# Row maxima of a softmax brought across partition quadrants: VectorE copies in place of a selector product on TensorE

## The chip, the cores and the metric

The kernel runs on one core of a Trainium2 chip. The metric is the device time of one execution in microseconds. Before the change it is 1114.38 us, the median of three runs (1112.85 to 1114.99).

## The reference

Attention with keys and values pooled over 4x4 windows, followed by a soft mixture of experts on its output. Sizes: B = 4 batches, N = 12288 queries per batch, C = 128 channels, 768 pooled keys per batch, 8 experts with 4 slots each.

```python
kv_pool = kv.reshape(B, H // r, r, W // r, r, C).mean(axis=(2, 4))
k = v = kv_pool.reshape(B, -1, C) @ w_sr
s = scale * (q @ k.transpose(0, 2, 1))
s = s - s.max(-1, keepdims=True)
a = np.exp(s)
a /= a.sum(-1, keepdims=True) + 1e-09
attn = a @ v
...
logits = x @ phi            # x: the attention's output, 49152 rows
d = softmax of logits over the rows;   slots = d.T @ x
slot_out = relu(slots @ w1) @ w2       # per expert
c = softmax of logits over the slots;  out = c @ slot_out
```

The maximum that matters here is `s.max(-1)`: one number per query, over its 768 keys.

## The kernel before, in words

The 49152 queries are worked through in 96 blocks of 512. A block's scores are computed transposed: TensorE multiplies six tiles of 128 keys with the 512 queries, in three products each (high and low parts of both operands, L473 to L475), so that keys lie on the partitions and queries along the free dimension. The six tiles fill three double banks of PSUM (s0 to s2).

The maximum over the keys is then a maximum across partitions. It is found in steps on VectorE:

- rowmax1, L480, three times per block: a transposing reduction of a double bank. It transposes 32x32 squares and takes the maximum along 32 keys. What comes out has, on partition j of quadrant k (a quadrant is a group of 32 partitions), for each of the block's 16 groups of 32 queries (NBK = 16) the maximum over the 32 keys that lie in quadrant k, for query j of the group.
- rowmax2, L490 and L492: the maximum over the six tiles (96 to 16 elements per partition, written to the top of a PSUM bank), then a product with `quad`, a 0/1 table, that spreads the 16 values of each quadrant into a slot of its own: 64 elements per partition, three quarters of them zeros.
- rowmax_pe, L500: TensorE multiplies these 128x64 values with `sel`, a 128x128 table of zeros and ones that adds up the partitions of equal number within their quadrant. Since only one of the four is not zero in each slot, every partition gets all four quadrants' maxima. It is an fp32 product, which the profile shows as two matmuls and two weight loads.
- rowmax3, L505: the maximum over the four slots (64 to 16 elements).
- rowmax4, L510: a transpose of 32x32 squares, which spreads the result so that every key's partition holds the maximum of each of the 512 queries (tile mb).

Then VectorE subtracts mb from the scores in four instructions (L518, tile t), which frees the double banks for the next block's products; ScalarE takes the exponential twice, to fp16 (phi, L525) and to fp32 (L529); GpSimd takes the difference of the two as a low part (plo, L534); and TensorE multiplies with the values in 72 matmuls (L551, L552, L559). GpSimd also splits the queries (qlo, L463). Every four blocks a group's logits are worked into a running softmax over the rows on all engines. After the last block comes the experts' part and the output.

The order of the instructions on TensorE, VectorE, ScalarE and GpSimd is written out by a planner (class Plan). Each step has an engine, a cost, a latency after it, a due time, the steps it needs and the buffers that it takes and gives back; the planner goes through time and always issues the most urgent step that can start. Due times of a block count from T0 = HEAD + i * PER. A step marked hot is waited for, up to HOLD = 0.7 us, instead of starting another on its engine. The steps of the maximum are hot: r2 (L935), pe (L936), r3 (L937), r4 (L938). Two PSUM banks (ring "m") are shared by the products with the values, the key and value projections, the groups' small products and the selector product; the planner lets the latter use the top of a bank beside a product with the values (key "pq").

Each engine executes its instructions in the order that the planner gave them, and waits at each for the results that it needs.

Of the kernel before, what the change touches and what calls it, by code (L numbers as in the profile page):

```python
# [11 lines left out]
F16 = mybir.dt.float16  # L12
U32 = mybir.dt.uint32
AF = mybir.ActivationFunctionType
ALU = mybir.AluOpType
X = mybir.AxisListType.X
# [3 lines left out]
P = 128  # L20
EPS = 1e-9
PK = 16.0
KSPLIT = 512
VK = 4096.0
Q32 = 32
# [7 lines left out]
class Plan:  # L33
# [13 lines left out]
    def op(self, eng, cost, lat, prio, deps, fn, acq=(), use=(), at=0.0, slack=0.0, hot=False, raw=0.0):  # L47
        n = len(self.ops)
        if eng != "PE" and any(ring == "m" for ring, _ in use):
            prio -= URGE  # L50
        for key in list(acq) + list(use):
            self.users.setdefault(key, []).append(n)
        self.ops.append((eng, cost, lat, prio, list(deps), fn, list(acq), at, slack, hot, raw, list(use)))
        return n
# [117 lines left out]
def attention_then_soft_moe(ctx: ExitStack, tc: tile.TileContext, qT, kv0, kvT, w_sr, w_srT, phi, w1, w2, outT):  # L172
    nc = tc.nc
    B, C, NQ = qT.shape
    R2, NK = kvT.shape[2], kvT.shape[3]
    NT = NK // P
    NS = phi.shape[1]
    E, _, FF = w1.shape
# [3 lines left out]
    BQ = 512  # L182
# [16 lines left out]
    TH = NT // NH  # L199
    PB = 5  # L200
# [7 lines left out]
    sp = es.enter_context(tc.tile_pool(name="sp", bufs=2))  # L208
# [16 lines left out]
        out=mask, in_=ident.rearrange("p (t e j) -> p e t j", t=TS, e=E), axis=XY, op=ALU.add  # L225
# [10 lines left out]
    NQD = P // Q32  # L236
    sel1 = cp.tile([P, Q32], F32, tag="sel1", name="sel1")
    nc.vector.tensor_reduce(out=sel1, in_=ident.rearrange("p (k j) -> p j k", k=NQD), axis=X, op=ALU.add)
    sel = cp.tile([P, P], F32, tag="sel", name="sel")
# [3 lines left out]
    quad = cp.tile([P, NQD], F32, tag="quad", name="quad")  # L243
# [14 lines left out]
    qsp = {}  # L258
    S = {}
    MX = {}  # L260
    PQ = {}
    TT_ = {}
    PP = {}
    PX = {}
# [3 lines left out]
    NBK = BQ // Q32  # L268
    NU = NT // 2

    plan = Plan({
        "m": 2, "t": TBUF, "phi": PB, "plo": PB, "q": 2, "qs": 2, "xl": 2, "D": 1, "kv": 2,
        "pooled": 1, "v32": 1, "r6": 2, "rq": 2, "m1": 2, "mb": 1, **{f"s{u}": 1 for u in range(NU)},
    })
    op = plan.op

    banks = [pm.tile([P, 512], F32, tag=f"m{b}", name=f"m{b}") for b in range(2)]
# [1 line left out]
    def mt(shape, name):  # L279
        return banks[plan.bank]  # L280

    PER = 9.8
    KLAG = 6
    KV0 = 14.5
    KVS = 1.0
    QKP = 5
# [197 lines left out]
        )  # L484

    def rowmax2(i):
        top = banks[plan.bank][:, 512 - (NQD + 1) * NBK :]
        pq = PQ[i] = top[:, NBK:]
        r1 = top[:, :NBK]
        nc.vector.tensor_reduce(out=r1, in_=MX[i].rearrange("p t b -> p b t"), axis=X, op=ALU.max)  # L490
        rq = sp.tile([P, NQD, NBK], F32, tag="rq", name=f"rq_{i}")
        nc.vector.tensor_tensor(  # L492
            out=rq, in0=r1.unsqueeze(1).broadcast_to([P, NQD, NBK]),
            in1=quad.unsqueeze(2).broadcast_to([P, NQD, NBK]), op=ALU.mult,
        )
        MX[i] = rq

    def rowmax_pe(i):
        pqv = PQ.pop(i)
        nc.tensor.matmul(pqv, sel, MX[i].rearrange("p k b -> p (k b)"), start=True, stop=True)  # L500
        MX[i] = pqv

    def rowmax3(i):
        m1 = sp.tile([P, NBK], F32, tag="m1", name=f"m1_{i}")
        nc.vector.tensor_reduce(out=m1, in_=MX[i].rearrange("p (k b) -> p b k", k=NQD), axis=X, op=ALU.max)  # L505
        MX[i] = m1

    def rowmax4(i):
        m = sp.tile([P, BQ], F32, tag="mb", name=f"mb_{i}", bufs=1)
        nc.vector.transpose(out=m, in_=MX[i].unsqueeze(2).broadcast_to([P, NBK, Q32]))  # L510
        MX[i] = m
# [9 lines left out]
        )  # L521

    def exp_hi(i, h):
        hi = PP[i, h] = sp.tile([P, TH, BQ], F16, tag="phi", name=f"phi_{i}_{h}", bufs=PB)
        nc.scalar.activation(hi, TT_[i, h], AF.Exp, bias=lnk, scale=SCALE)  # L525

    def exp_t(i, h):
# [3 lines left out]
    def plo(i, h):  # L531
        lo = sp.tile([P, TH, BQ], F16, tag="plo", name=f"plo_{i}_{h}", bufs=PB)
        eng = nc.vector if i == NB - 1 else nc.gpsimd
        eng.tensor_tensor(out=lo, in0=TT_.pop((i, h)), in1=PP[i, h], op=ALU.subtract)  # L534
        PP[i, h] = (PP[i, h], lo)

    def av_tile(i, k):
        if k % 2 == 0 and i == NB - 1:
# [6 lines left out]
    def av_hi(i, k):  # L545
        _, vhi, vlo = VU[i // BPB]
        px = av_tile(i, k)
        ks = slice(k * P, (k + 1) * P)
        for t in range(NT):
            p = PP[i, t // TH][0][:, t % TH, ks]  # L550
            nc.tensor.matmul(px, p, vhi[:, t, :], start=(t == 0), stop=False)  # L551
            nc.tensor.matmul(px[:, 1:], p, vlo[:, t, :], start=False, stop=False)  # L552

    def av_lo(i, k):
        vhi = VU[i // BPB][1]
        px = PX[i, k // 2][:, k % 2, :]
        ks = slice(k * P, (k + 1) * P)
        for t in range(NT):
            nc.tensor.matmul(px, PP[i, t // TH][1][:, t % TH, ks], vhi[:, t, :], start=False, stop=(t == NT - 1))  # L559
# [195 lines left out]
    def dve(n):  # L755
        return n / 960 + 0.07
# [15 lines left out]
    ops = {}  # L772
# [19 lines left out]
    for n, which in enumerate(LOADS):  # L792
        dep = [] if n < 2 else [ops["pool", 0, 6 * (n - 1) - 2]]
        loaded.append(op("SP", 0.3, 0, 0, dep, lambda which=which: start_kv(which)))
        for h, e0, cnt in which:
            for c in range(e0, e0 + cnt, 2):
# [4 lines left out]
                    acq=[("t", ("pool", h))] if c == 0 else [], use=[("t", ("pool", h))] if c else [],  # L801
# [96 lines left out]

    def av_rest(i, k, m, p, prev):
        los = [ops["lo", i, 0], ops["lo", i, 1]]  # L900
        a2 = op("PE", 6 * 0.072, 0.17, p + 0.8, prev + los, lambda: av_lo(i, k), use=[("plo", (i, 0)), ("plo", (i, 1)), m])
        if k % 2:
            g = GOF[i]
            first = i == GB[g][0] and k == 1
            x = ("xl", g)
            ops["x", i, k // 2] = op(
                "DVE" if i == NB - 2 and k == 1 else "ACT", act(2 * VW) + (0.1 if i == NB - 2 and k == 1 else -0.03), 0.1, p - 2, [a2] + evs[-1:], lambda: av_evac(i, k // 2),
                acq=[x] if first else [], use=[m] + ([] if first else [x]),
            )
            evs.append(ops["x", i, k // 2])  # L910
        return [a2]
# [3 lines left out]
    for i in range(NB):  # L915
        b, ib = divmod(i, BPB)
        T0 = HEAD + i * PER
# [5 lines left out]
        kd = [ops["k", b, 0], ops["k", b, 1]]  # L923
        for t in range(NT):
            u = t // 2
            ops["qk", i, t] = op(
                "PE", 3 * 0.2315, 0.17, T0 - QKP + 0.65 * t, [ops["ql", i]] + kd[: 1 if t < KSPLIT // P else 2] + ([ops["qk", i, t - 1]] if t else [ops["qk", i - 1, NT - 1]] if i else []),
                lambda i=i, t=t: qk(i, t), acq=[(f"s{u}", i)] if t % 2 == 0 else [], use=[("qs", i)] + ([(f"s{u}", i)] if t % 2 else []),
            )
            if t % 2:  # L930
                ops["r", i, u] = op(
                    "DVE", dve(2 * BQ) + 0.02, 0.08, T0 - 2.0 + 0.65 * t, [ops["qk", i, t], ops["qk", i, t - 1]] + ([ops["r", i, u - 1]] if u else []),
                    lambda i=i, u=u: rowmax1(i, u), acq=[("r6", i)] if u == 0 else [], use=[(f"s{u}", i)] + ([("r6", i)] if u else []),
                )
        r2 = op("DVE", 0.36, 0.08, T0 + 2, [ops["r", i, NU - 1]], lambda i=i: rowmax2(i), acq=[("m", ("pq", i)), ("rq", i)], use=[("r6", i)], hot=True, raw=0.14)  # L935
        pe = op("PE", 0.27, 0.3, T0 - 10, [r2], lambda i=i: rowmax_pe(i), use=[("m", ("pq", i)), ("rq", i)], hot=True)  # L936
        r3 = op("DVE", 0.12, 0.08, T0 - 10, [pe], lambda i=i: rowmax3(i), acq=[("m1", i)], use=[("m", ("pq", i))], hot=True)  # L937
        r4 = op("DVE", dve(BQ) - 0.03, 0.08, T0 - 10, [r3], lambda i=i: rowmax4(i), acq=[("mb", i)], use=[("m1", i)], hot=True, raw=0.14)  # L938
        for t, n in ((0, 2), (2, 1), (3, 1), (4, 2)):
            h, o2 = divmod(t, TH)  # L940
            ops["s", i, t] = op(
                "DVE", dve(n * BQ), 0.08, T0 - 4 + 0.63 * t, [r4] + ([ops["s", i, t0]] if t else []), lambda i=i, t=t, n=n: sub(i, t, n),
                acq=[("t", (i, h))] if o2 == 0 else [], use=[(f"s{t // 2}", i), ("mb", i)] + ([("t", (i, h))] if o2 else []),
                raw=0.0 if t else 0.14,
# [3 lines left out]
        for h in range(NH):  # L948
# [5 lines left out]
                acq=[("plo", (i, h))], use=[("t", (i, h)), ("phi", (i, h))],  # L954
            )
            ops["hi", i, h] = e1
        prev = [ops["hi", i, 0], ops["hi", i, 1], ops["t", b, 0], ops["t", b, 1]] + ([ops["av", i - 1]] if i else []) + ([ops["g7m", GOF[i] - 2]] if i == GB[GOF[i]][0] and GOF[i] > 1 else [])
        los = [ops["lo", i, 0], ops["lo", i, 1]]
        pp = [("phi", (i, 0)), ("phi", (i, 1))]
        pl = [("plo", (i, 0)), ("plo", (i, 1))]  # L960
        end = i == NB - 1
        px = [(f"s{k // 2}" if end else "m", ("px", i, k // 2)) for k in range(TB)]
        for k in range(TB):
            m = px[k]
            p = T0 + AVD * PER + 1.3 * k
            a1 = op("PE", 12 * 0.0705, 0.17, p, prev + ([] if end else los), lambda i=i, k=k: av_hi(i, k), acq=[m] if k % 2 == 0 else [], use=pp + ([m] if k % 2 else []))
            ops["hv", k] = prev = [a1]
            if not end:
                prev = av_rest(i, k, m, p, prev)
        if end:  # L970
            for k in range(TB):
                prev = av_rest(i, k, px[k], T0 + AVD * PER + 6, prev)
        a2 = prev[0]
# [28 lines left out]
    for g in range(len(GB)):  # L1002
        n = nt(g) * NS
        p = HEAD + (GB[g][0] + GB[g][1] + KLAG) * PER
# [230 lines left out]
```

## Time and profile before

| | |
|---|---|
| median of three runs | 1114.38 us |
| the profiled execution's own time | 1114.22 us |
| its span, first to last instruction | 1112.4 us |
| TensorE, VectorE busy, share of the span | 94%, 89% |
| ScalarE, GpSimd busy, share of the span | 74%, 78% |

A group's line in the profile reads: line of the kernel, engine, operation, what is written and read, shapes (partitions x elements), number of instructions, then busy time in us and mean ns of one, then the idle time of the engine just before them and what ended it. PE is TensorE, PEld its weight loads, DVE VectorE, ACT ScalarE, POOL GpSimd. In the view of waits a line names who waited for whom, the total, how many times and the longest. In the timeline a row has its start and its length in us. The view of busy time by window has one column per engine, in the order PE, PEld, DVE, ACT, POOL, then the granted clock, the busy share of the DMA engines and GB/s.

### The profile page before, as it was taken

Reading aid. Unit: us, or ns where it says so; the run is one execution under the profiler, and the core shown is the slowest. Engines: PE = TensorE matmul, PEld = TensorE weight load, DVE = VectorE, ACT = ScalarE, POOL = GpSimd, SP = SyncE. Lnnn points to the kernel's source line nnn. Section 1 sums busy time; section 2 is a strip of 40 time slices with the busy share of each in tenths; the row PEclk is TensorE's granted clock in tenths of the full one; section 3 lists DMA queues with packets and bytes.
Section 4 is the critical chain, followed back from the end, with each engine's and each line's share of the span. In section 5 each row is a group of like instructions: output and inputs, shape, how many; then the busy total and the mean of one; then the engine's idle time right before and its main releaser. Section 6 shows DMA issues by size and latency. Waiting matters only on the chain.

```text
span 1112.4 us, 24632 instructions
## 1 busy us (share of the span) xinstructions
PE 1046.7 (94%) x10198; PEld 897.3 (81%) x10198; DVE 984.9 (89%) x1492; ACT 822.7 (74%) x1006; POOL 866.2 (78%) x480
## 2 busy tenths in 40 slices
PE   3699999999999999999999999999999999997876
PEld 2588888888888888888888888888888888886343
DVE  7899889889889989899899988989989988987895
ACT  1677778778778778878877788688788777875563
POOL 0579897788899888789889889779889889773340
PEclk9799999999999999999999999999999999999885
DMA  9315421111125310120136210120110110113398
GB/s 342 117 22 132 96 44 39 39 58 39 39 54 124 91 42 22 39 70 27 39 83 123 71 53 1 39 96 2 39 39 1 39 39 2 39 39 115 141 407 360
DMA packets 17407, 89.15 MB, mean 80 GB/s; under 512 B 1680, under 2 KB 3984, under 8 KB 11152
## 3 DMA queue, kind: packets, MB, share of 16 engines
q1 hardware_dynamic: 13408, 69.47, 16.8%
q0 software_dynamic: 3312, 17.70, 8.4%
q8 instruction: 81, 1.33, 0.5%
q10 hardware_dynamic: 576, 0.41, 0.1%
q14 instruction: 30, 0.25, 0.1%
HBM read 58.87 MB, written 25.17 MB: 76 GB/s over the span
## 4 chain that ended last, share of the span: by engine, by line
PE 67%; DVE 27%; issue 2%; ACT 2%; POOL 1%; DMA 1%; SPq 0%; DVEq 0%; ACTq 0%; POOLq 0%
PE m L551 11%; PE m L552 10%; PE m L559 10%; PE s L473 9%; PE s L475 9%; PE s L474 9%; DVE t L518 8%; DVE r L480 8%; PE m L500 3%; PE m L690 2%; DVE mb L510 2%; PE po L1120 2%; DVE o L1129 2%; DVE cm L628 1%; DVE pool L311 1%
## 5 line engine op out<-in xcount | busy, mean ns | idle before, releaser
L534 POOL TENSOR_TENSOR plo<-t,phi 128x1536 f16<-128x1536 f32 x190 | 595.8, 3143 | 125.1 <-ACT t L529 123.8
L525 ACT ACTIVATE phi<-t,lnk 128x1536 f16<-128x1536 f32 x192 | 301.6, 1571 | 133.5 <-DVE t L518 132.9
L480 DVE TRANSPOSE_TENSOR_REDUCE r<-s 128x32 f32<-128x1024 f32 x288 | 349.8, 1236 | 27.1 <-PE s L475 21.1
L551 PE MATMUL m<-vhi,phi 128*128 128x161 f16 x2280 | 354.5, 234 | 2.5 <-DVE m L505 1.3
L552 PE MATMUL m<-vlo,phi 128*128 128x160 f16 x2280 | 353.5, 233 | 0.0
L518 DVE TENSOR_TENSOR t<-s,mb 128x1024 f32<-128x1024 f32 (+1 forms) x384 | 342.9, 949 | 8.8 <-DVE mb L510 0.9
L529 ACT ACTIVATE t<-t,lnk 128x1536 f32<-128x1536 f32 x192 | 299.8, 1568 | 2.3
L551 PEld LDWEIGHTS <-phi 128*128 128x128 f16 x2304 | 227.0, 99 | 22.9 <-issue 22.8
L473 PE MATMUL s<-qhi,khi 128*128 128x512 f32 x576 | 238.1, 413 | 6.5 <-DVE t L518 6.1
L552 PEld LDWEIGHTS <-phi 128*128 128x128 f16 x2304 | 225.5, 98 | 5.2 <-issue 3.3
L475 PE MATMUL s<-qhi,klo 128*128 128x512 f32 x576 | 227.2, 394 | 0.0
L474 PE MATMUL s<-qlo,khi 128*128 128x512 f32 x576 | 226.6, 393 | 0.0
L559 PE MATMUL m<-vhi,plo 128*128 128x161 f16 x2280 | 221.9, 233 | 0.3 <-POOL plo L534 0.3
L559 PEld LDWEIGHTS <-plo 128*128 128x128 f16 x2304 | 174.8, 100 | 1.3 <-issue 0.6
L463 POOL TENSOR_TENSOR qlo<-q,qhi 128x512 fp32r<-128x512 f32 x96 | 125.7, 1310 | 26.9 <-ACT qhi L459 26.9
L569 ACT ACTIVATE xl<-m 128x322 f32<-128x322 f32 x189 | 81.0, 428 | 76.1 <-PE m L559 75.7
L473 PEld LDWEIGHTS s<-qhi,khi 128*128 128x128 f32 x576 | 109.7, 190 | 29.9 <-issue 3.6
L475 PEld LDWEIGHTS s<-qhi,klo 128*128 128x128 f32 x576 | 109.2, 190 | 24.6 <-DVE klo L353 0.5
L474 PEld LDWEIGHTS s<-qlo,khi 128*128 128x128 f32 x576 | 109.8, 191 | 20.3 <-issue 0.7
L510 DVE STREAM_TRANSPOSE mb<-m 128x512 f32<-128x512 f32 x96 | 68.3, 711 | 3.3
L459 ACT ACTIVATE qhi<-q 128x512 fp32r<-128x512 f32 x96 | 59.2, 617 | 2.4 <-issue 1.0
L505 DVE TENSOR_REDUCE m<-m 128x16 f32<-128x64 f32 x96 | 21.5, 224 | 40.5 <-PE m L500 40.5
(140 smaller groups left out, 854.1 us busy)
## 6 DMA issues: line engine op xcount, KB each, us to landing
q<-qT SPq DMA_DIRECT2D x23, 1024.0 KB, 4.8
outT<-o SPq DMA_DIRECT2D x21, 1024.0 KB, 5.2
kva<-kvT POOLq DMA_DIRECT2D x9, 1536.0 KB, 11.4
kva<-kvT SPq DMA_DIRECT2D x3, 1536.0 KB, 10.5
kv<-kv SPq DMA_DIRECT2D x8, 512.0 KB, 5.7
w<-w SPq DMA_DIRECT2D x2, 1536.0 KB, 6.4
w<-w SPq DMA_DIRECT2D x4, 768.0 KB, 4.6
outT<-o SPq DMA_DIRECT2D x6, 512.0 KB, 4.3
```

The lines of the kernel that those rows point to most:

```text
L463: nc.gpsimd.tensor_tensor(out=lo, in0=q_src(i), in1=hi.bitcast(F32), op=ALU.subtract)
L473: nc.tensor.matmul(s, khi[:, ks], hi, start=True, stop=False)
L474: nc.tensor.matmul(s, khi[:, ks], lo, start=False, stop=False)
L475: nc.tensor.matmul(s, klo[:, ks], hi, start=False, stop=True)
L480: nc.vector.tensor_reduce(out=MX[i][:, 2 * u : 2 * u + 2, :].rearrange("p t b -> p (t b)"), in_=S[i, u].rearrange("p t (b j) -> p (t b) j" ...
L518: nc.vector.tensor_tensor(out=TT_[i, h][:, o : o + n, :], in0=S[i, t // 2][:, u : u + n, :], in1=MX[i].unsqueeze(1).broadcast_to([P, n, BQ ...
L525: nc.scalar.activation(hi, TT_[i, h], AF.Exp, bias=lnk, scale=SCALE)
L529: nc.scalar.activation(t, t, AF.Exp, bias=lnk, scale=SCALE)
L534: eng.tensor_tensor(out=lo, in0=TT_.pop((i, h)), in1=PP[i, h], op=ALU.subtract)
L551: nc.tensor.matmul(px, p, vhi[:, t, :], start=(t == 0), stop=False)
L552: nc.tensor.matmul(px[:, 1:], p, vlo[:, t, :], start=False, stop=False)
L559: nc.tensor.matmul(px, PP[i, t // TH][1][:, t % TH, ks], vhi[:, t, :], start=False, stop=(t == NT - 1))
```

## The change

The product with `quad` and the selector product are gone. L490 writes its 16 maxima into slot 0 of an SBUF tile rq on all 128 partitions. Three copies on VectorE bring the values of partitions 32 to 63, 64 to 95 and 96 to 127 down to slots 1, 2 and 3 of partitions 0 to 31. Four reductions on VectorE then each read the four slots of partitions 0 to 31 and write their maximum to one of the four quadrants of m1. The transpose L510 follows as before. TensorE has no part in the maximum any more, and nothing of it lies in the shared PSUM banks.

The planner's table follows: the step pe is gone, r2, r3 and r4 have new costs, the period of the due times PER is 9.5 instead of 9.8, and the assumed costs of the products are slightly lower. The handle of a block's phi (PP) becomes a pair from the start, so that the last block's first products may be issued ahead of its low parts.

```diff
-    PER = 9.8
+    PER = 9.5
...
     def rowmax2(i):
-        top = banks[plan.bank][:, 512 - (NQD + 1) * NBK :]
-        pq = PQ[i] = top[:, NBK:]
-        r1 = top[:, :NBK]
-        nc.vector.tensor_reduce(out=r1, in_=MX[i].rearrange("p t b -> p b t"), axis=X, op=ALU.max)
         rq = sp.tile([P, NQD, NBK], F32, tag="rq", name=f"rq_{i}")
-        nc.vector.tensor_tensor(
-            out=rq, in0=r1.unsqueeze(1).broadcast_to([P, NQD, NBK]),
-            in1=quad.unsqueeze(2).broadcast_to([P, NQD, NBK]), op=ALU.mult,
-        )
+        nc.vector.tensor_reduce(out=rq[:, 0, :], in_=MX[i].rearrange("p t b -> p b t"), axis=X, op=ALU.max)
+        for k in range(1, NQD):
+            nc.vector.tensor_copy(rq[:Q32, k, :], rq[k * Q32 : (k + 1) * Q32, 0, :])
         MX[i] = rq
-
-    def rowmax_pe(i):
-        pqv = PQ.pop(i)
-        nc.tensor.matmul(pqv, sel, MX[i].rearrange("p k b -> p (k b)"), start=True, stop=True)
-        MX[i] = pqv
 
     def rowmax3(i):
         m1 = sp.tile([P, NBK], F32, tag="m1", name=f"m1_{i}")
-        nc.vector.tensor_reduce(out=m1, in_=MX[i].rearrange("p (k b) -> p b k", k=NQD), axis=X, op=ALU.max)
+        for k in range(NQD):
+            nc.vector.tensor_reduce(
+                out=m1[k * Q32 : (k + 1) * Q32, :], in_=MX[i][:Q32].rearrange("p k b -> p b k"), axis=X, op=ALU.max
+            )
         MX[i] = m1
...
-        hi = PP[i, h] = sp.tile([P, TH, BQ], F16, tag="phi", name=f"phi_{i}_{h}", bufs=PB)
+        hi = sp.tile([P, TH, BQ], F16, tag="phi", name=f"phi_{i}_{h}", bufs=PB)
+        PP[i, h] = (hi, None)
...
-        a2 = op("PE", 6 * 0.072, 0.17, p + 0.8, prev + los, lambda: av_lo(i, k), use=[("plo", (i, 0)), ("plo", (i, 1)), m])
+        a2 = op("PE", 6 * 0.070, 0.17, p + 0.8, prev + los, lambda: av_lo(i, k), use=[("plo", (i, 0)), ("plo", (i, 1)), m])
...
-                "PE", 3 * 0.2315, 0.17, T0 - QKP + 0.65 * t, [ops["ql", i]] + kd[: 1 if t < KSPLIT // P else 2] + ([ops["qk", i, t - 1]] if t else [ops["qk", i - 1, NT - 1]] if i else []),
+                "PE", 3 * 0.2275, 0.17, T0 - QKP + 0.65 * t, [ops["ql", i]] + kd[: 1 if t < KSPLIT // P else 2] + ([ops["qk", i, t - 1]] if t else [ops["qk", i - 1, NT - 1]] if i else []),
...
-        r2 = op("DVE", 0.36, 0.08, T0 + 2, [ops["r", i, NU - 1]], lambda i=i: rowmax2(i), acq=[("m", ("pq", i)), ("rq", i)], use=[("r6", i)], hot=True, raw=0.14)
-        pe = op("PE", 0.27, 0.3, T0 - 10, [r2], lambda i=i: rowmax_pe(i), use=[("m", ("pq", i)), ("rq", i)], hot=True)
-        r3 = op("DVE", 0.12, 0.08, T0 - 10, [pe], lambda i=i: rowmax3(i), acq=[("m1", i)], use=[("m", ("pq", i))], hot=True)
-        r4 = op("DVE", dve(BQ) - 0.03, 0.08, T0 - 10, [r3], lambda i=i: rowmax4(i), acq=[("mb", i)], use=[("m1", i)], hot=True, raw=0.14)
+        r2 = op("DVE", 0.46, 0.08, T0 + 2, [ops["r", i, NU - 1]], lambda i=i: rowmax2(i), acq=[("rq", i)], use=[("r6", i)], hot=True, raw=0.1)
+        r3 = op("DVE", 0.4, 0.08, T0 - 10, [r2], lambda i=i: rowmax3(i), acq=[("m1", i)], use=[("rq", i)], hot=True, raw=0.18)
+        r4 = op("DVE", dve(BQ) + 0.03, 0.08, T0 - 10, [r3], lambda i=i: rowmax4(i), acq=[("mb", i)], use=[("m1", i)], hot=True, raw=0.18)
...
-            a1 = op("PE", 12 * 0.0705, 0.17, p, prev + ([] if end else los), lambda i=i, k=k: av_hi(i, k), acq=[m] if k % 2 == 0 else [], use=pp + ([m] if k % 2 else []))
+            a1 = op("PE", 12 * 0.0695, 0.17, p, prev + ([] if end else los), lambda i=i, k=k: av_hi(i, k), acq=[m] if k % 2 == 0 else [], use=pp + ([m] if k % 2 else []))
```

More of the change, by code (lines that the diff above doesn't have):

```diff
@@ L260, in attention_then_soft_moe @@
     MX = {}
-    PQ = {}
     TT_ = {}
@@ L533, in plo @@
         eng = nc.vector if i == NB - 1 else nc.gpsimd
-        eng.tensor_tensor(out=lo, in0=TT_.pop((i, h)), in1=PP[i, h], op=ALU.subtract)
-        PP[i, h] = (PP[i, h], lo)
+        eng.tensor_tensor(out=lo, in0=TT_.pop((i, h)), in1=PP[i, h][0], op=ALU.subtract)
+        PP[i, h] = (PP[i, h][0], lo)
     def av_tile(i, k):
```

## The prediction

> **What bounds the kernel now.** I read the page's span, engine and chain lines first, then the busy time from 60 to 960 us, where block follows block, and the view of the instructions on tile mb, which gives the length of a block.
>
> ```profile
> span 1112.4 us, 24632 instructions
> PE 1046.7 (94%) x10198; PEld 897.3 (81%) x10198; DVE 984.9 (89%) x1492; ACT 822.7 (74%) x1006; POOL 866.2 (78%) x480
> PE 67%; DVE 27%; issue 2%; ACT 2%; POOL 1%; DMA 1%; SPq 0%; DVEq 0%; ACTq 0%; POOLq 0%
> ...
> 60.00:960.00 900.00, 889.91 (x8872) 784.45 (x8871) 814.99 (x1197) 707.51 (x840) 777.59 (x414) 1.00 0.20 52
> ...
> L510 DVE STREAM_TRANSPOSE mb<-m x96: 711/711/714, 31.1 to 1004.3; 128x512 f32<-128x512 f32 x96
> ```
>
> L510 runs once in each of the 96 blocks, so a block takes (1004.3 - 31.1) / 95 = 10.244 us, and the 900 us hold 87.9 blocks. The first busy column is TensorE's: 889.91, so it is idle for 0.11 us per block, at a granted clock of 1.00. The third is VectorE's: 814.99 / 87.9 = 9.28 us of work per block, 0.97 idle. The last chain goes 67% over TensorE and 27% over VectorE. TensorE sets the pace and VectorE follows less than a microsecond behind: what is taken off TensorE counts until VectorE is full. The waits, and one block from the timeline, show where the two hold each other up.
>
> ```profile
> DVE m L505 <- PE m L500: 40.5, 74, 0.8
> ...
> DVE r L480 <- PE s L475: 21.1, 27, 1.7
> ...
> PEld m L500 <- DVE rq L492: 15.0, 28, 2.4
> ...
> PE m L500 <- DVE rq L492: 9.8, 24, 2.0
> ```
>
> ```profile
> 514.52 0.23 PE L551 MATMUL m<-vhi,phi 128*128 128x161 f16 x1
> ...
> 514.59 0.23 PE L552 MATMUL m<-vlo,phi 128*128 128x160 f16 x1
> 514.81 0.22 DVE L492 TENSOR_TENSOR rq<-m,quad 128x64 f32<-128x64 f32 x1
> 514.95 0.67 DVE L701 TENSOR_REDUCE RM<-LL 128x16 f32<-128x512 f32 x1
> ...
> 515.09 0.43 PE L500 MATMUL m<-rq,sel 128*128 128x64 f32 x2 [0.26 <-DVE rq L492]
> ...
> 515.36 0.58 PE L559 MATMUL m<-vhi,plo 128*128 128x161 f16 x6
> 515.56 0.22 DVE L505 TENSOR_REDUCE m<-m 128x16 f32<-128x64 f32 x1
> ```
>
> **What goes.** The selector product leaves TensorE. Its matmuls start 0.07 us apart (514.52, 514.59), so L559 could have started at 514.66; it started at 515.36. That is 0.70 us lost, of which 515.36 - 515.09 = 0.27 is the product itself and the rest is waiting for L492. Where TensorE doesn't wait, 0.27 is all. Without it, TensorE's block is between 10.24 - 0.70 = 9.54 and 10.24 - 0.27 = 9.97 us. From VectorE go L492, L505 (0.22 us each) and L505's wait, 40.5 / 96 = 0.42 us per block. The places in the two PSUM banks that L490 and L500 wrote are free too; I count nothing for that, since neither bank appears in the waits above as anything but this product.
>
> **What comes.** Three copies of 32x16 and four maxima over 32x64 on VectorE, and L490 writes SBUF, not PSUM. None of these is in the trace; the rows nearest in size are these.
>
> ```profile
> L490 DVE TENSOR_REDUCE m<-r 128x16 f32<-128x96 f32 x96 | 31.5, 328 | 5.8
> L630 DVE TENSOR_REDUCE cmt<-cm 128x1 f32<-128x16 f32 x23 | 3.9, 170 | 0.8
> L583 DVE TENSOR_SCALAR acc<-acc,al 128x129 f32<-128x129 f32 x1 | 0.3, 289 | 0.0
> L240 DVE COPY sel<-sel 128x128 f32<-128x128 f32 x1 | 0.2, 217 | 0.0
> ```
>
> ```profile
> 990.20 3.12 POOL L534 TENSOR_TENSOR plo<-t,phi 128x1536 f16<-128x1536 f32 x1 [3.19 <-ACT t L529]
> ...
> 990.78 0.21 DVE L606 RECIPROCAL r<-xl 128x16 f32<-128x16 f32 x1
> ...
> 992.25 0.33 DVE L490 TENSOR_REDUCE m<-r 128x16 f32<-128x96 f32 x1
> ...
> 992.62 0.22 DVE L492 TENSOR_TENSOR rq<-m,quad 128x64 f32<-128x64 f32 x1
> ...
> 993.27 1.07 POOL L623 TENSOR_TENSOR LL<-xl,ru 128x512 f32<-128x512 f32 x1
> 993.43 0.22 DVE L505 TENSOR_REDUCE m<-m 128x16 f32<-128x64 f32 x1 [0.59 <-PE m L500]
> ...
> 993.69 0.71 DVE L510 STREAM_TRANSPOSE mb<-m 128x512 f32<-128x512 f32 x1
> ...
> 994.29 3.14 POOL L534 TENSOR_TENSOR plo<-t,phi 128x1536 f16<-128x1536 f32 x1
> ```
>
> L701 started 0.14 us after L492, which took 0.22: an instruction that needs nothing of the one before overlaps it by 0.08. One that needs its result starts after its end: L490 takes 0.33 and L492 starts 0.37 after it, so 0.03 to 0.04 lies between. A copy of 16 elements costs at most the 0.17 us of L630; the three cost 0.09 + 0.09 + 0.17 = 0.35. A maximum over 64 elements is L505's size; the four cost 3 x 0.14 + 0.22 = 0.64. L490 may stay at 0.33 or, freed of its PSUM output, fall towards L505's 0.22: I allow 0 to 0.08. VectorE's work per block becomes 9.28 - 0.22 - 0.22 + 0.35 + 0.64 = 9.83, or 9.75. I take 9.79.
>
> The path itself gets no shorter. From the start of L490 to that of L510 it was 993.69 - 992.25 = 1.44 us; now it is 0.36 (L490) + 0.38 (copies) + 0.67 (maxima) = 1.41. What changes is that TensorE isn't interrupted and VectorE doesn't stand still in the middle. Nothing can be put in the old pause any more (L701 filled it in the block above), but in the sum over busy time that is contained already.
>
> VectorE is now the fuller engine (9.79 against TensorE's 9.54 to 9.97). Of its idle 0.97 us the 0.42 at L505 go. L480's wait for TensorE, 21.1 / 96 = 0.22, shrinks as TensorE gets ahead; the remaining 0.33 are pauses of 0.03 between dependent instructions and the group's hand-overs. I keep 0.18 (about half of those) for what TensorE's own 9.54 to 9.97 can't hide. A block then takes 9.97 us, 0.27 less than now, and 95 of them 26 us less. Head and tail are not touched. The span would be 1086; the profiled run's own time was 1114.22, 1.82 over its span, and 0.16 under the median of 1114.38, so the forecast is 1088 us. Its bounds: a block of 9.70 (VectorE's work at 9.51, if the seven small instructions cost 0.04 less each than their nearest rows, with 0.19 idle) gives 1062; a block of 10.20 (all of the 0.33 and a third of L480's wait stay) gives 1110.
>
> What is next late is the rest of VectorE: behind the copies, which wait for L490, and the maxima, which wait for the copies, stand L510 and the four L518, on which ScalarE's exponentials and TensorE's next L473 wait. The planner's due times (PER 9.8 to 9.5) and costs only change the order of ready work; DMA engines are busy for a share of 0.20 in the window above, which hides any shift of a load, and the 1.82 us outside the span isn't touched. The change of PP lets the last block's products come before its plo; it adds no instruction.
>
> **Rival: no overlap between quadrants.** Every VectorE instruction in the rows above starts at partition 0. The copies read from partitions 32, 64 and 96 and the maxima write there. If an instruction that changes its quadrant starts only when the one before is done, 2 + 3 overlaps of 0.08 go, 0.40 us, and up to 0.03 is added at each: 0.40 to 0.55, on VectorE, which is then the bound. A block takes 9.97 + 0.45 = 10.42, the kernel 1088 + 0.45 x 95 = 1131 us (1100 to 1162 with the bounds above). It decides from 0.27 us. For it speaks nothing in the trace; against it nothing either. [...] No run here shows it yet.
>
> **Rival: the copies wait for GpSimd.** This is the expensive one. In the head, one VectorE addition of two SBUF operands met a GpSimd instruction:
>
> ```profile
> 9.87 1.22 DVE L311 TENSOR_TENSOR pool<-pool,kv 128x1024 f32<-128x1024 f32 x1
> ...
> 10.67 1.54 POOL L463 TENSOR_TENSOR qlo<-q,qhi 128x512 fp32r<-128x512 f32 x1 [9.14 <-ACT qhi L459]
> 11.13 3.42 DVE L311 TENSOR_TENSOR pool<-pool,kv 128x1024 f32<-128x1024 f32 x2
> ...
> 13.33 3.74 DVE L311 TENSOR_TENSOR pool<-pool,kv 128x1024 f32<-128x1024 f32 x3
> ```
>
> L463 ended at 12.21. The L311 of 11.13 took until 13.33, 2.20 us in place of 1.22: about a microsecond more, as if it had started at 12.21. So some VectorE instructions wait for a whole GpSimd instruction. Would a copy? [...] Against it stands L606: 16 elements from SBUF to SBUF at 990.78, amid the L534 of 990.20 to 993.32, in 0.21 us. If copies wait, the first one (at L492's place, 992.62) waits until 993.32 and finds L623 and the L534 of 994.29 queued back to back behind; a copy that loses to each of them costs 0.70 + 1.07 + 3.14 = 4.9 us, one that loses to the running instruction alone 0.70. It decides from the 0.27 us that there are to lose. With 0.70 the kernel takes 1088 + 0.70 x 95 = 1155, with 4.9 some 1550; I take the middle, one running and one short instruction (1.8 us), 1259 us. [...]
>
> **Rival: nothing to gain.** If VectorE's 0.97 us of idle is all of other waits, L505's 0.42 comes back elsewhere and a block stays at 10.24: 1114.
>
> **How the numbers follow.** The nearest row to a small copy or maximum beside GpSimd is L606, which neither waited nor stretched; so the forecast, 1088, gets 0.57. The quadrants get 0.19 (1131), GpSimd's wait 0.17 (1259), nothing to gain 0.07. The forecast's own range is 1062 to 1110. The range for 8 in 10 takes in nearly all of the quadrant case, up to 1142, and leaves out the GpSimd case (0.17) and 0.03 at the ends. Below 1114 by over 0.2% (2 us, what a measurement of this kernel can tell from none): the forecast and the low end of the quadrant case (0.02), 0.59; within it 0.07; above it the rest of the quadrants and GpSimd's wait, 0.17 + 0.17 = 0.34.
>
> **What would show it.** Right: L500 gone; copies at or below 0.17 us and starting 0.06 to 0.10 apart; maxima 0.14 apart; L490 to L510 near 1.4 us; blocks near 9.97; VectorE's idle share halved and TensorE's idle time up. Quadrants: the same instructions starting 0.17 and 0.22 or more apart, and L490 to L510 near 1.9. GpSimd: copies of a microsecond and more that end with a POOL instruction. Wrong altogether: blocks of 10.24 with VectorE waiting elsewhere.

## The result and the profile after

The changed kernel takes 1570.21 us (median of four runs, 1565.01 to 1572.09) against 1114.68 us for the kernel before on the same chip: the ratio is 1.409, 95% interval 1.4066 to 1.4113. It is slower by 456 us. The forecast was 1088 us; the case that came true is the one called "the copies wait for GpSimd", which had a chance of 0.17 and was put at 1259 us.

From the page of the changed kernel, the lines that answer to those of before:

```profile
span 1568.6 us, 24657 instructions
PE 1166.5 (74%) x10006; PEld 971.9 (62%) x10006; DVE 1390.8 (89%) x1972; ACT 834.3 (53%) x1006; POOL 865.4 (55%) x480
...
DVE 59%; PE 37%; issue 3%; DMA 1%; ACT 1%; POOL 0%; SPq 0%; DVEq 0%; ACTq 0%
DVE rq L489 22%; PE s L472 12%; DVE r L479 11%; PE s L473 10%; PE s L474 10%; DVE t L510 8%; DVE m L495 6%; DVE mb L502 4%; DVE rq L487 2%; PE m L552 2%; PE po L1112 1%; DVE o L1121 1%; DVE RM L694 1%; DMA kv<-kv 1%; PE m L1090 1%
...
L489 DVE COPY rq<-rq 32x16 f32<-32x16 f32 x288 | 347.0, 1205 | 5.9
L495 DVE TENSOR_REDUCE m<-rq 32x16 f32<-32x64 f32 x384 | 95.9, 250 | 7.2
```

(In the changed kernel the lines move: L487 is the first reduction, L489 the copies, L495 the four maxima, L502 the transpose, L510 the subtractions, L479 the transposing reductions, L472 to L474 the score products.) VectorE's share stayed at 89%, but what it is busy with has changed: 288 copies of 16 elements take 347.0 us, 1205 ns each. The nearest row of before had promised 170. TensorE fell from 94% to 74%, and the chain went from 67% TensorE to 59% VectorE, with 22% of the span in the copies alone. A busy engine isn't a working one here: the profile counts the shortest of these copies as busy for 161 ns and the longest for 4051, of the same 16 elements, and its waits name nothing that a copy waited for.

What it waits for stands in the timeline, both engines together, and then the single copies in narrow windows of it:

```profile
712.59 1.05 POOL L616 TENSOR_TENSOR LL<-xl,ru 128x512 f32<-128x512 f32 x1
...
713.31 3.66 DVE L489 COPY rq<-rq 32x16 f32<-32x16 f32 x3
713.61 3.09 POOL L527 TENSOR_TENSOR plo<-t,phi 128x1536 f16<-128x1536 f32 x1
716.65 0.12 POOL L431 MEMSET vhi<- 128x6 f16 x1
717.01 1.04 DVE L495 TENSOR_REDUCE m<-rq 32x16 f32<-32x64 f32 x4
```

```profile
713.31 0.36 DVE L489 COPY rq<-rq 32x16 f32<-32x16 f32 x1
...
713.69 3.10 DVE L489 COPY rq<-rq 32x16 f32<-32x16 f32 x1
...
716.81 0.17 DVE L489 COPY rq<-rq 32x16 f32<-32x16 f32 x1
```

GpSimd's L616 ends at 713.64 and the first copy at 713.67; the second copy takes 3.10 us and ends at 716.79, when GpSimd's L527 (to 716.70) and the short L431 behind it (to 716.77) are done; the third meets an idle GpSimd and takes 0.17. Over all 288 copies, 175 took over 0.3 us, and each of these ended 22 to 36 ns after the end of a GpSimd instruction. Of the 113 others only two lie wholly inside the time of a GpSimd TENSOR_TENSOR.

The rest of the loss shows in the waits, on TensorE and back:

```profile
PE s L472 <- DVE t L510: 337.0, 92, 9.5
...
DVE r L479 <- PE s L474: 104.6, 120, 1.7
```

In the kernel before, the first of these waits was

```profile
PE s L473 <- DVE t L518: 6.1, 3, 3.4
```

TensorE stands idle for 337 us waiting for the subtractions that free the score banks (6.1 before). And VectorE waits 104.6 us for the scores themselves, against 21.1 before. The granted clock has dropped:

```profile
60.00:1400.00 1340.00, 1016.09 (x8836) 864.37 (x8834) 1206.71 (x1667) 726.63 (x848) 789.61 (x420) 0.87 0.13 35
```

It is 0.87 where it was 1.00.

### The profile page after: what moved, and what is told of

Its sections match the earlier page's. It is cut to its first block, busy times and chain, and to the rows that moved or that the text cites. A ratio compares the mean times of both kernels' runs of the same rounds, so it can differ in the third digit from the quotient of the medians.

```text
span 1568.6 us, 24657 instructions
## 1 busy us (share of the span) xinstructions
PE 1166.5 (74%) x10006; PEld 971.9 (62%) x10006; DVE 1390.8 (89%) x1972; ACT 834.3 (53%) x1006; POOL 865.4 (55%) x480
## 4 chain that ended last, share of the span: by engine, by line
DVE 59%; PE 37%; issue 3%; DMA 1%; ACT 1%; POOL 0%; SPq 0%; DVEq 0%; ACTq 0%
DVE rq L489 22%; PE s L472 12%; DVE r L479 11%; PE s L473 10%; PE s L474 10%; DVE t L510 8%; DVE m L495 6%; DVE mb L502 4%; DVE rq L487 2%; PE m L552 2%; PE po L1112 1%; DVE o L1121 1%; DVE RM L694 1%; DMA kv<-kv 1%; PE m L1090 1%
## 5 line engine op out<-in xcount | busy, mean ns | idle before, releaser
L527 POOL TENSOR_TENSOR plo<-t,phi 128x1536 f16<-128x1536 f32 x190 | 592.3, 3117 | 506.6 <-ACT t L522 469.2
L472 PE MATMUL s<-qhi,khi 128*128 128x512 f32 x576 | 297.3, 516 | 337.3 <-DVE t L510 337.0
L479 DVE TRANSPOSE_TENSOR_REDUCE r<-s 128x32 f32<-128x1024 f32 x288 | 357.7, 1245 | 113.4 <-PE s L474 104.6
L472 PEld LDWEIGHTS s<-qhi,khi 128*128 128x128 f32 x576 | 142.3, 247 | 385.3 <-issue 349.6
L489 DVE COPY rq<-rq 32x16 f32<-32x16 f32 x288 | 347.0, 1205 | 5.9
L510 DVE TENSOR_TENSOR t<-s,mb 128x1024 f32<-128x1024 f32 (+1 forms) x384 | 342.6, 948 | 6.9
L473 PE MATMUL s<-qlo,khi 128*128 128x512 f32 x576 | 277.1, 481 | 0.0
L474 PE MATMUL s<-qhi,klo 128*128 128x512 f32 x576 | 272.2, 473 | 0.0
L552 PE MATMUL m<-vhi,plo 128*128 128x161 f16 x2280 | 234.4, 241 | 0.0
L474 PEld LDWEIGHTS s<-qhi,klo 128*128 128x128 f32 x576 | 139.7, 243 | 36.3
L473 PEld LDWEIGHTS s<-qlo,khi 128*128 128x128 f32 x576 | 141.5, 246 | 27.5 <-issue 0.7
L495 DVE TENSOR_REDUCE m<-rq 32x16 f32<-32x64 f32 x384 | 95.9, 250 | 7.2
```

The costliest lines, as they stand in the source:

```text
L472: nc.tensor.matmul(s, khi[:, ks], hi, start=True, stop=False)
L473: nc.tensor.matmul(s, khi[:, ks], lo, start=False, stop=False)
L474: nc.tensor.matmul(s, klo[:, ks], hi, start=False, stop=True)
L479: nc.vector.tensor_reduce(out=MX[i][:, 2 * u : 2 * u + 2, :].rearrange("p t b -> p (t b)"), in_=S[i, u].rearrange("p t (b j) -> p (t b) j" ...
L489: nc.vector.tensor_copy(rq[:Q32, k, :], rq[k * Q32 : (k + 1) * Q32, 0, :])
L510: nc.vector.tensor_tensor(out=TT_[i, h][:, o : o + n, :], in0=S[i, t // 2][:, u : u + n, :], in1=MX[i].unsqueeze(1).broadcast_to([P, n, BQ ...
```

## The experiments

**Theory A**, after the result: a copy with both ends in SBUF waits for the GpSimd instruction that is running. **Rival B**: it is the move to another quadrant that is slow. The first four kernels take one thing at a time out of the changed kernel.

**1. The same move by another operation.** The one-element maximum has the operands of the copy to the byte.

```diff
-            nc.vector.tensor_copy(rq[:Q32, k, :], rq[k * Q32 : (k + 1) * Q32, 0, :])
+            nc.vector.tensor_reduce(
+                out=rq[:Q32, k, :], in_=rq[k * Q32 : (k + 1) * Q32, 0, :].unsqueeze(2), axis=X, op=ALU.max
+            )
```

> The three copies become maxima over a single element (same operands, same partitions, same SBUF tile), everything else as in the changed kernel. Theory A (a copy between SBUF operands waits for the GpSimd instruction that is running, a reduction doesn't): each takes about 0.2 us instead of the 1.205 of the copies, none ends with a GpSimd instruction, and the kernel falls from 1570 to about 1145 us (1115 to 1175), since the four maxima still take the 1.04 us of the changed kernel's timeline. Theory B (moving data to another quadrant is what is slow): they stay near 1.2 us and the time near 1570.

Measured: 1146.88 us, ratio to before 1.0296 (1.0278 to 1.0313). The groups of this kernel, and the view of its line 489 (shortest, median and longest in ns):

```profile
L497 DVE TENSOR_REDUCE m<-rq 32x16 f32<-32x64 f32 x384 | 96.9, 252 | 7.3
L504 DVE STREAM_TRANSPOSE mb<-m 128x512 f32<-128x512 f32 x96 | 68.3, 711 | 3.3
L489 DVE TENSOR_REDUCE rq<-rq 32x16 f32<-32x16 f32 x288 | 45.6, 158 | 5.9
```

```profile
L489 DVE TENSOR_REDUCE rq<-rq x288: 156/158/163, 29.8 to 1035.3; 32x16 f32<-32x16 f32 x144
```

None of 288 took longer than 163 ns, and not for want of GpSimd: 257 of them lie wholly inside the time of a running GpSimd TENSOR_TENSOR. 423 of the 456 us are gone by the choice of the operation alone; the planner's new table is still in this kernel, so it isn't what cost them. Rival B falls: crossing quadrants doesn't cost a microsecond.

**2. The same operation without the move.** The copies read quadrant 0, so the maxima cover a quarter of the keys.

```diff
-            nc.vector.tensor_copy(rq[:Q32, k, :], rq[k * Q32 : (k + 1) * Q32, 0, :])
+            nc.vector.tensor_copy(rq[:Q32, k, :], rq[:Q32, 0, :])
```

> The three copies read partitions 0 to 31 instead of 32 to 127, so nothing crosses a quadrant and the maxima are those of a quarter of the keys. Theory A (wait for GpSimd): the copies still take 1.0 to 1.3 us in the mean and the time stays at 1530 to 1600 us. Theory B (crossing is slow): copies of 0.2 us or less and 1115 to 1175 us.

Measured once: 1302 us, between the two. The copies still wait, up to 3.1 us, but the mean is 627 ns, half:

```profile
L489 DVE COPY rq<-rq x288: 154/194/3145, 29.9 to 1191.5; 32x16 f32<-32x16 f32 x144
```

In the order of the three the means are 558, 272 and 1051 ns: it is the second that now seldom waits (its median is 155 ns). In the changed kernel they are 705, 971 and 1938. A block of the timeline, then its first and third copy in narrow windows:

```profile
620.15 1.44 DVE L489 COPY rq<-rq 32x16 f32<-32x16 f32 x3
620.51 1.05 POOL L664 TENSOR_TENSOR D<-D,rv 128x512 f32<-128x512 f32 x1
```

```profile
620.15 0.42 DVE L489 COPY rq<-rq 32x16 f32<-32x16 f32 x1
...
620.57 1.02 DVE L489 COPY rq<-rq 32x16 f32<-32x16 f32 x1
```

The first waits for the GpSimd instruction that is running (to 620.55), the second overlaps the end of the first, and the third, which starts at 620.57, ends at 621.59, when the next GpSimd instruction (620.51 to 621.56) is done. So A holds, but I missed that the quadrants matter for the wait too. In all 96 blocks of this kernel each copy starts 77 to 80 ns before the one ahead of it ends; in the changed kernel, where each copy changes quadrant, it starts 13 or 14 ns after that end. What this has to do with the wait wasn't tried by itself. Neither theory's number was right.

**3. The same copies out of PSUM.** The first reduction writes to the top of a PSUM bank, as before the change; four copies bring the values from there.

```diff
-        nc.vector.tensor_reduce(out=rq[:, 0, :], in_=MX[i].rearrange("p t b -> p b t"), axis=X, op=ALU.max)
-        for k in range(1, NQD):
-            nc.vector.tensor_copy(rq[:Q32, k, :], rq[k * Q32 : (k + 1) * Q32, 0, :])
+        r1 = banks[plan.bank][:, 512 - NBK :]
+        nc.vector.tensor_reduce(out=r1, in_=MX[i].rearrange("p t b -> p b t"), axis=X, op=ALU.max)
+        for k in range(NQD):
+            nc.vector.tensor_copy(rq[:Q32, k, :], r1[k * Q32 : (k + 1) * Q32, :])
...
```

In the planner's table, r2 takes the top of a shared bank again.

> The first reduction writes its 16 values to the top of a shared PSUM bank, as the kernel before did, and four copies (quadrant 0 too) bring them from PSUM to the SBUF slots. Theory A in its narrow form (only copies with both ends in SBUF wait for GpSimd): copies of 0.17 to 0.2 us, and with one instruction more than with maxima about 1165 us (1130 to 1200). If every copy of VectorE waits for GpSimd, or crossing quadrants is slow: 1570 us or more.

Measured: 1171.68 us, ratio 1.0519 (1.0503 to 1.0535).

```profile
L490 DVE COPY rq<-m x384: 161/168/176, 29.9 to 1060.2; 32x16 f32<-32x16 f32 x192
```

Not one of 384 copies waited, though 357 of them lie wholly inside a GpSimd TENSOR_TENSOR. It is neither the name of the operation nor the quadrant alone that waits, but a copy with both ends in SBUF.

**4. Shorter GpSimd instructions.** Each low part is made in three instructions of 512 elements.

```diff
-        eng.tensor_tensor(out=lo, in0=TT_.pop((i, h)), in1=PP[i, h][0], op=ALU.subtract)
+        t = TT_.pop((i, h))
+        for j in range(TH):
+            eng.tensor_tensor(out=lo[:, j, :], in0=t[:, j, :], in1=PP[i, h][0][:, j, :], op=ALU.subtract)
```

> GpSimd makes each low part in three instructions of 512 elements instead of one of 1536; the copies of the changed kernel are kept. Theory A: a copy waits for at most about 1.1 us (one short instruction) instead of 3.1, the mean copy falls from 1.205 to 0.5 to 0.8 us, and the time falls to 1250 to 1430 us although GpSimd's work grows. Theory B, or any theory without GpSimd: the copies keep their 1.2 us and the time 1570 or more.

Measured once: 1436 us, just above the range.

```profile
L489 DVE COPY rq<-rq x288: 161/1098/5550, 29.9 to 1321.7; 32x16 f32<-32x16 f32 x144
```

The median copy now takes 1098 ns, close to the length of one short GpSimd instruction (1159 ns in the median). Only one copy took over 1.4 us, against 84 in the changed kernel; that one took 5.55 us, over a GpSimd DMA issue and the four instructions queued behind it, so the 1.1 us expected as the most one copy waits doesn't hold for every copy. The mean falls only from 1205 to 875: with short instructions queued back to back more copies lose to one (235 of 288 took over 0.3 us, 175 in the changed kernel). The direction is A's; mean and time both lie just above what was expected.

**5. The quadrants by themselves.** As in experiment 1, but all seven small instructions stay on partitions 0 to 31. The maxima of three quarters of the keys are left out; the other partitions of the tile m1c, which the transpose reads, hold zeros.

```diff
...
-                out=rq[:Q32, k, :], in_=rq[k * Q32 : (k + 1) * Q32, 0, :].unsqueeze(2), axis=X, op=ALU.max
+                out=rq[:Q32, k, :], in_=rq[:Q32, 0, :].unsqueeze(2), axis=X, op=ALU.max
...
-                out=m1[k * Q32 : (k + 1) * Q32, :], in_=MX[i][:Q32].rearrange("p k b -> p b k"), axis=X, op=ALU.max
+                out=x1[:Q32, k, :] if k < NQD - 1 else m1[:Q32, :], in_=MX[i][:Q32].rearrange("p k b -> p b k"), axis=X, op=ALU.max
```

> As with maxima in place of the copies, but all seven small instructions read and write partitions 0 to 31 only (the fourth maximum writes the tile that the transpose reads, whose other partitions hold zeros), so the maxima of three quarters of the keys are left out and the output isn't the reference's. Theory C (an instruction that changes quadrant starts only when the one before is done): the four maxima fall from 1.04 us to about 0.67, the three small ones from 0.53 to 0.35, blocks get shorter by 0.5 to 0.6 us and the kernel runs in about 1097 us (1085 to 1115), near the forecast of 1088. Rival D (small instructions on 32 partitions take 0.25 us whatever they touch): no change, 1140 to 1150.

Measured: 1106.74 us, ratio 0.9935 (0.992 to 0.995). One block of this kernel, then one of experiment 1:

```profile
600.66 0.32 DVE L490 TENSOR_REDUCE rq<-r 128x16 f32<-128x96 f32 x1
601.01 0.31 DVE L492 TENSOR_REDUCE rq<-rq 32x16 f32<-32x16 f32 x3
601.36 0.59 DVE L499 TENSOR_REDUCE x<-rq 32x16 f32<-32x64 f32 x3
601.87 0.24 DVE L499 TENSOR_REDUCE m1c<-rq 32x16 f32<-32x64 f32 x1
602.14 0.71 DVE L506 STREAM_TRANSPOSE mb<-m1c 128x512 f32<-128x512 f32 x1
```

```profile
601.52 0.32 DVE L487 TENSOR_REDUCE rq<-r 128x16 f32<-128x96 f32 x1
601.88 0.50 DVE L489 TENSOR_REDUCE rq<-rq 32x16 f32<-32x16 f32 x3
602.41 1.05 DVE L497 TENSOR_REDUCE m<-rq 32x16 f32<-32x64 f32 x4
603.50 0.71 DVE L504 STREAM_TRANSPOSE mb<-m 128x512 f32<-128x512 f32 x1
```

In one quadrant three small maxima take 0.31 us and the four larger ones 0.75 (601.36 to 602.11); across quadrants 0.50 and 1.05. That is three and four whole lengths one after the other: 3 x 0.158 and 4 x 0.252 are 0.47 and 1.01. Theory C is shown, at 0.49 us in this block and, from experiment 1's 10.580 us per block to this one's 10.169, 0.41 us in the mean.

**6. TensorE's clock.** The changed kernel with extra matmuls where TensorE waits. A first attempt wrote them to a shared bank of its own:

```diff
+    def warm(i):
+        pw = mt([P, 512], f"warm_{i}")
+        for j in range(14):
+            kh = kT[(i - 1) // BPB][0]
+            nc.tensor.matmul(pw, kh[:, :P], kh[:, :512], start=True, stop=True)
...
```

> The changed kernel with 14 extra fp32r matmuls of 128x512 on TensorE ahead of each block's score products, where it stands idle for VectorE; their results aren't used. Theory E (a part of the loss comes from TensorE's granted clock, 0.87 in the steady part against 1.00 before, because TensorE now idles for microseconds in each block): the clock rises to 0.97 or more, VectorE's wait for the score products (104.6 us in all) falls by half or more, and the time falls from 1570 to 1450 to 1530 us. Rival: the slower clock is hidden behind the copies' waits: 1560 to 1620.

Measured once: 1715 us, outside both expected ranges. The clock rose only to 0.93 (60 to 1400 us), and the time can't be put down to it: the extra matmuls themselves waited for the bank, 91.4 us for ScalarE's L568 and 57.0 for VectorE's L650, and VectorE's wait for the scores rose to 254.2 us. The second attempt needs no bank of its own:

```diff
+    def warm(i):
+        pw = banks[plan.bank][:, 512 - C - NS :]
+        v = VU[(i - 3) // BPB][1]
+        for j in range(36):
+            nc.tensor.matmul(pw, v[:, j % NT, 1 : C + 1], v[:, j % NT, 1:], start=True, stop=True)
...
```

> The changed kernel with 36 short extra fp16 matmuls (128x160) ahead of each block's score products from the fifth block on, written to the unused top of a shared PSUM bank, so that they need no bank of their own; their results aren't used. Theory E (the falling TensorE clock is part of the loss): the clock in the steady part rises from 0.87 to 0.95 or more, VectorE's wait for the score products falls from 104.6 us to under 60, and the time falls to 1480 to 1550 us. Rival (the slower products are covered, and the extra matmuls only get in the way): 1565 us or more with the wait for the scores unchanged or longer.

Measured once: 1521 us. Its steady part, its copies and its wait:

```profile
60.00:1400.00 1340.00, 1185.08 (x12475) 1057.08 (x12473) 1249.17 (x1726) 750.33 (x881) 815.06 (x433) 0.97 0.14 36
```

```profile
L495 DVE COPY rq<-rq 32x16 f32<-32x16 f32 x288 | 348.1, 1209 | 5.9
```

```profile
DVE r L485 <- PE s L474: 58.5, 68, 1.7
```

The clock is back at 0.97, the copies are as slow as ever (1209 ns), the wait for the scores fell by 46 us and the time by 49, with more work on TensorE. So the lower clock is a second loss that grows out of the first; in this one run some 49 of the 456 us came back with it. The extra matmuls also shift other work on TensorE, and the clock didn't quite reach 1.00, so 49 us is an estimate of the clock's share. Two other runs with part of the copies' waits lie in between: from 60 to 1000 us the clock was 0.95 in experiment 2 and 0.91 in experiment 4; in experiment 1, where none of the small maxima took longer than 163 ns, it was 1.00.

**7. One maximum and a spreading.** From experiment 1, in place of four maxima:

```diff
+        nc.vector.tensor_reduce(out=m1[:Q32, :], in_=MX[i][:Q32].rearrange("p k b -> p b k"), axis=X, op=ALU.max)
+        for k in range(1, NQD):
+            nc.vector.tensor_reduce(out=m1[k * Q32 : (k + 1) * Q32, :], in_=m1[:Q32, :].unsqueeze(2), axis=X, op=ALU.max)
```

> With maxima in place of the copies, and then one maximum on partitions 0 to 31 and three one-element maxima that spread its 16 values to the other quadrants, in place of four maxima of 64 elements. If each of these instructions costs its whole length because it changes quadrant, four of 0.26 us become one of 0.28 and three of 0.17 to 0.19: 0.2 us less per block, 1128 us (1120 to 1136). If the quadrants aren't what sets their cost, the new dependence between the maximum and its spreading takes the gain back: 1143 to 1150.

Measured: 1123.88 us, ratio 1.0087 (1.0063 to 1.0111). One block:

```profile
599.92 0.50 DVE L489 TENSOR_REDUCE rq<-rq 32x16 f32<-32x16 f32 x3
600.46 0.25 DVE L496 TENSOR_REDUCE m<-rq 32x16 f32<-32x64 f32 x1
600.74 0.51 DVE L498 TENSOR_REDUCE m<-m 32x16 f32<-32x16 f32 x3
```

The maximum and its spreading take 601.25 - 600.46 = 0.79 us, where the four maxima of experiment 1 took 1.05: the cost went by whole lengths, as C has it. It is the best way found here to cross quadrants on VectorE, and still slower than the selector product.

**8. A cheaper selector product.** The kernel before, with its product in one pass.

```diff
+    selr = cp.tile([P, P], F32R, tag="selr", name="selr")
...
+    nc.vector.tensor_copy(selr, sel)
...
-        rq = sp.tile([P, NQD, NBK], F32, tag="rq", name=f"rq_{i}")
+        rq = sp.tile([P, NQD, NBK], F32R, tag="rq", name=f"rq_{i}")
...
-        nc.tensor.matmul(pqv, sel, MX[i].rearrange("p k b -> p (k b)"), start=True, stop=True)
+        nc.tensor.matmul(pqv, selr, MX[i].rearrange("p k b -> p (k b)"), start=True, stop=True)
```

> The kernel before, with the selector and the tile rq in fp32r, so that the selector product is one matmul and one weight load instead of two of each (the maxima are rounded, which a softmax allows, since the same rounded number is subtracted from all keys). If TensorE's interruption of 0.27 us and VectorE's wait of 0.42 us per block are what the selector product costs, half the product gives back 0.1 to 0.2 us per block: 1095 to 1107 us. If they are hidden: 1112 to 1117.

Measured: 1103.21 us, ratio 0.9903 (0.9887 to 0.992), the fastest of all. The product's group and VectorE's wait for it:

```profile
L502 PE MATMUL m<-rq,selr 128*128 128x64 f32 x96 | 26.9, 280 | 10.5 <-DVE rq L494 9.9
```

```profile
DVE m L507 <- PE m L502: 29.8, 71, 0.5
```

96 matmuls instead of 192, and a wait of 29.8 us instead of 40.5. Keeping the crossing on TensorE and halving it gains no less than the VectorE version without either of its two losses (experiment 5, 0.992 to 0.995).

## Why the prediction was wrong, step by step

**The step that failed** is the choice between two rows for a price that the trace didn't have: "The nearest row to a small copy or maximum beside GpSimd is L606, which neither waited nor stretched; so the forecast, 1088, gets 0.57." L606 was near in size and place, but it is another operation. The row that showed a wait had been read and set back: L311 took about a microsecond longer beside GpSimd (2.17 us in a window of its own; the prediction's 2.20 is from start to start). L311 is an addition of two SBUF operands and no copy, so the trace of before left the question open; preferring the row that didn't wait was the mistake. Experiments 1, 3 and 4 decide it: a copy between SBUF operands waits for GpSimd (1205 ns in the mean in the changed kernel, 875 beside shorter GpSimd instructions), a reduction (158) and a copy from PSUM (168) don't. In the prediction's sum, the 0.35 us for the three copies were 3 x 1.205 = 3.61. The runs show which instructions wait and for what, not why.

**The size of that rival.** It was priced at 0.70 to 4.9 us per block, 1.8 taken. The copies cost 3 x (1.205 - 0.158) = 3.14 us per block more than the maxima that replace them. The bounds held and the 1.8 was too low; what the prediction saw in one block (a running instruction, then one queued behind it, then another) is what happens. Two things came on top. Blocks take (1458.6 - 33.5) / 95 = 15.00 us, 4.42 more than in experiment 1:

```profile
L502 DVE STREAM_TRANSPOSE mb<-m x96: 711/711/714, 33.5 to 1458.6; 128x512 f32<-128x512 f32 x96
```

```profile
L504 DVE STREAM_TRANSPOSE mb<-m x96: 711/711/714, 31.4 to 1036.5; 128x512 f32<-128x512 f32 x96
```

```profile
DVE r L479 <- PE s L474: 3.9, 6, 0.8
```

3.14 are the copies; 1.05 is VectorE's longer wait for the scores (104.6 us against 3.9 in experiment 1, over 96), of which the filler matmuls won back 46 us, 0.48 per block, with the clock; 0.23 I can't place. The prediction took the clock of 1.00 as given; with TensorE busy for 1016 of 1340 us it was 0.87.

**The quadrants.** This was a rival with a chance of 0.19, priced at 0.40 to 0.55 us per block; 0.41 was measured. From L487 to the transpose it takes 603.50 - 601.52 = 1.98 us in experiment 1, where "near 1.9" was named. The mechanism was there as well, hidden under the larger one. The two weren't exclusive, though the prediction gave them chances as if they were.

**What was right.** VectorE's work without both mechanisms was put at 9.79 us per block. Experiment 5 is that kernel: its window holds 940 / 10.169 = 92.4 blocks, so 907.68 / 92.4 = 9.82.

```profile
60.00:1000.00 940.00, 913.80 (x9178) 795.98 (x9176) 907.68 (x1726) 742.25 (x882) 816.63 (x434) 1.00 0.19 51
```

The copies that took the least time, 161 ns in the changed kernel, and those out of PSUM in experiment 3, 168 in the mean, cost what was taken from L630 (170). L490's PSUM output was worth next to nothing (322 ns into SBUF in experiment 5, 328 before; 0 to 0.08 us had been allowed). The idle time was too small: 0.18 us per block was kept, 0.35 remained, so that even this kernel takes 1107 us, not 1088. TensorE didn't need the whole time it was given: in that window it idles for (940 - 913.80) / 92.4 = 0.28 us per block, where 0.11 was before.

## What to carry to other kernels

Before a small VectorE instruction is priced by its size, look at its operation and at where both its ends lie: beside a busy GpSimd a copy from SBUF to SBUF often cost what was left of a GpSimd instruction, in the longest case (4.05 us) with the one behind it, and the same move as a one-element maximum (156 to 163 ns) or from PSUM (161 to 176 ns) did not. When a trace has no row for an operation, a row that shares only its size doesn't settle its price: L606 took 0.21 us, the copies 1.205 in the mean. On a kernel whose engines are all nearly full, halving the cost of a step where it stands (0.9903) may beat moving it to another engine (1.0087 at best).

## What the runs showed of the hardware beyond that

VectorE copies that change quadrant started 13 or 14 ns after the one ahead ended, copies within a quadrant 77 to 80 ns before it. Copies that stay in one quadrant lost to GpSimd less often (135 of 288 took over 0.3 us, 627 ns in the mean, against 175 and 1205); in the block shown the third copy, 1.02 us long, ended 0.03 us after a GpSimd instruction that had started at 620.51, 0.06 us before the first copy ended. TensorE's granted clock fell as it was made to wait: 1.00 in the steady part of the kernel before, 0.87 in that of the changed kernel, 0.97 with filler matmuls, and the filler paid for itself with 49 us. Why the third of the copies in one quadrant still waits (1051 ns in the mean) was not tried.
